# Even and odd columns apart: another layout for the moving operands of a spectral layer and a feed-forward network

## The chip, the core and the metric

The kernel runs on one core of a Trainium2 chip, in a single launch. The metric is the device time of one execution in microseconds, the median of several runs. The core has a matrix engine (TensorE, PE in the profile; its weight loads are shown as an engine of their own, PEld), a vector engine (VectorE, DVE), a scalar engine (ScalarE, ACT), GpSimd (POOL), and a sequencer that issues most transfers (SyncE, SP). Matrix products read both operands from the on-chip memory SBUF and write to PSUM.

## The reference

Eight sequences of 3008 tokens with 256 features go through a Fourier layer and then through a feed-forward network:

```python
X = np.fft.rfft(x, axis=1)
Yr = Xr @ w_r - Xi @ w_i + b_r          # float32
Yi = Xr @ w_i + Xi @ w_r + b_i
Y  = softshrink(Yr, 0.01) + 1j * softshrink(Yi, 0.01)
y  = np.fft.irfft(Y, n=3008, axis=1)     # 8 x 3008 x 256
h  = y @ w_in                            # 24064 x 2048
g  = h - np.tanh(h)
out = g @ w_out                          # 24064 x 256
```

`w_in` and `w_out` arrive as float64.

## The kernel before

**Arithmetic.** The precise products are made of three fp32r products. A float32 operand is split into a rounded high part (`_h`, written by ACT as fp32r) and the rest (`_l`, a subtraction on DVE, also written as fp32r), and the product is low·high + high·high + high·low, added up in PSUM. A few products near the start and two transforms (L361, L580) run in full float32; each of these shows as two matmul records in the trace, while an fp32r product shows as one.

**The Fourier part** is done batch by batch in small matrices (3008 = 64 · 47). Class `Stacked` (L278) makes the first transform of batches 1 to 7: `split` rounds a tile `xs` of 94 rows by 2 x 256 columns, `dft` (L301) multiplies it, ACT copies the result out of PSUM into `st` (L304), and a DMA stores `st` to DRAM. Class `Spectrum` makes the second transform, the complex linear layer, the shrinkage and the first half of the inverse; `Chunk.wave` and `Chunk.fold` make the second half of the inverse and leave `yt`, the network's input, with features on the partitions and tokens along the columns.

**The network** works on 52 chunks of tokens, 44 of 470 columns and 8 of 424. `halves` (L598) splits `yt` into `yh` and `yl`. For each of 16 blocks `f` of 128 hidden units, `up` makes six matmuls (L609: `win_l`·`yh`, `win_h`·`yh`, `win_h`·`yl`, two tiles of features each) into a PSUM tile `h`, then ACT makes `th` = tanh (L618), DVE `g` = `h` - `th` (L621), ACT `gh` (L624), DVE `gl` (L627). `down` makes six matmuls (L640: `gh` with `wout_l` and `wout_h`, `gl` with `wout_h`, for two halves of the output), added up over `f` in two PSUM tiles. A chunk and a block together are a slot; there are 832. The tiles `yh`, `yl`, `gh` and `gl` have rows of 512 words (`PITCH`), of which the first 470 or 424 are used, and every matmul reads them as one run of adjacent columns.

**Order.** It is written out by hand: in slot `g` the loop emits `up` of slot `g + 2`, then whatever of the Fourier part was put into this slot by `plan_stacked` and `plan_spectrum`, then `down` of slot `g`. So between the making of `gh` and `gl` and their use lie about two slots. `th`, `g`, `gh` and `gl` have three buffers each. The first slots also carry the conversion of the weights from float64 (class `Block`, L185 to L217), whose inputs are every second word of `w_raw`.

Of the kernel before, what the change touches and what calls it, by code (L numbers as in the profile page):

```python
# [10 lines left out]
F32 = mybir.dt.float32  # L11
# [3 lines left out]
ALU = mybir.AluOpType  # L15

B, S, D, FF = 8, 3008, 256, 2048
# [61 lines left out]
def spectral_ffn(ctx, tc, x, w_r, w_i, b_r, b_i, w_in, w_out, x_twice, f1, f1s, f2, i1, i2, out):  # L79
    nc = tc.nc  # L80
    P = 128
# [14 lines left out]
    ps_h = ctx.enter_context(tc.tile_pool(name="ps_h", bufs=2, space=PSUM))  # L96
    ps_o = ctx.enter_context(tc.tile_pool(name="ps_o", bufs=1, space=PSUM))
    ps_f = ctx.enter_context(tc.tile_pool(name="ps_f", bufs=4, space=PSUM))

    def split(src, name, pool=const, tag=None, bufs=None, rest=nc.vector):  # L100
        hi, lo = pair_like(src, name, pool, tag, bufs)
        split_into(hi, lo, src, rest)
        return hi, lo
# [119 lines left out]
    stack = {}  # L223
# [57 lines left out]
    class Stacked:  # L281
# [15 lines left out]

        def dft(self, q):
            ps = ps_f.tile([P, 512], F32, name="ps_f1", tag="f")
            pv = ps.rearrange("p (a d) -> p a d", d=D)  # L300
            nc.tensor.matmul(pv, stack["r"], self.xs[q], start=True, stop=True)  # L301
            if q == 0:
                self.st = work.tile([96, XC, D], F32, name="st", tag="st")
            nc.scalar.copy(out=self.st[:, 2 * q:2 * q + 2, :], in_=pv[:96])  # L304
            if 2 * q + 2 == XC:
                n = self.ch * XC
                nc.sync.dma_start(out=a_dram[self.b][n:n + XC].rearrange("n r d -> r n d"), in_=self.st)
# [18 lines left out]
    def halves(t, jp):  # L326
        v = t.rearrange("n (u g j) d -> u n g (j d)", u=2, j=NJ)
        return [v[u][:, :, 2 * jp * D:(2 * jp + 2) * D] for u in range(2)]

    class Spectrum:  # L330
# [6 lines left out]
        def load(self):  # L337
            if self.jp == 0:
                z_dram[self.b] = dram.tile([P * NJ, D], F32, name=f"z_{self.b}", tag="z")
            self.at = load.tile([P, 2, D], F32, name="at", tag="at", bufs=3)  # L340
            dst = self.at.rearrange("p j d -> p (j d)")
            if self.b < PAIRED:
                nc.sync.dma_start(out=dst, in_=rows(a_dram[self.b], self.jp))
                return
            first, second = halves(a_dram[self.b], self.jp)
            nc.sync.dma_start(out=dst, in_=first)
            n = 2 * XC * LOOK if self.b == PAIRED else 0
            nc.gpsimd.dma_start(out=dst[2 * n:], in_=second[n:], accum_op=ALU.add)  # L348
# [192 lines left out]
    class Chunk:  # L541
# [55 lines left out]

        def halves(self, t):  # L598
            n, y = self.n, self.y[t]
            nc.scalar.copy(out=self.yh[:, t, :n], in_=y[:, :n])  # L600
            nc.vector.tensor_tensor(out=self.yl[:, t, :n], in0=y[:, :n], in1=self.yh[:, t, :n].bitcast(F32), op=ALU.subtract)  # L601

        def up(self, f, between=()):
            n = self.n
            h = ps_h.tile([P, 512], F32, name="h", tag="h")
            k = 0
            for lhs, rhs in ((win_l, self.yh), (win_h, self.yh), (win_h, self.yl)):
                for t in range(2):
                    nc.tensor.matmul(h[:, :n], lhs[:, t, f * P:(f + 1) * P], rhs[:, t, :n], start=k == 0, stop=k == 5)  # L609
                    k += 1  # L610
            between = dict(enumerate(between))

            def fill(k):
                for op in between.get(k, ()):
                    op()

            th = ffn.tile([P, CT], F32, name="th", tag="th")
            nc.scalar.activation(out=th[:, :n], in_=h[:, :n], func=AF.Tanh)  # L618
            fill(0)
            g = ffn.tile([P, CT], F32, name="g", tag="g")  # L620
            nc.vector.tensor_tensor(out=g[:, :n], in0=h[:, :n], in1=th[:, :n], op=ALU.subtract)  # L621
            fill(1)
            gh = ffn.tile([P, PITCH], F32R, name="gh", tag="g_h")
            nc.scalar.copy(out=gh[:, :n], in_=g[:, :n])  # L624
            fill(2)
            gl = ffn.tile([P, PITCH], F32R, name="gl", tag="g_l")
            nc.vector.tensor_tensor(out=gl[:, :n], in0=g[:, :n], in1=gh[:, :n].bitcast(F32), op=ALU.subtract)  # L627
            fill(3)
            return gh, gl

        def down(self, f, gh, gl):
            n = self.n
            if f == 0:
                if self.c == 1:
                    self.o = [ps_f.tile([P, 512], F32, name=f"o{t}", tag="f") for t in range(2)]
                else:
                    self.o = [ps_o.tile([P, 512], F32, name=f"o{t}", tag=f"o{t}") for t in range(2)]
            for t in range(2):
                for k, (lhs, rhs) in enumerate(((wout_l, gh), (wout_h, gh), (wout_h, gl))):
                    nc.tensor.matmul(  # L640
                        self.o[t][:, :n], lhs[:, f, t * P:(t + 1) * P], rhs[:, :n],
                        start=f == 0 and k == 0, stop=f == NF - 1 and k == 2,
                    )

# [19 lines left out]
    with tc.manual_schedule(engines={E.PE, E.Activation, E.DVE, E.Pool, E.SP}):  # L664
# [21 lines left out]
        for i in range(len(steps) + 1):  # L686
            if i < len(steps):
                steps[i][0].whole(steps[i][1])
            if i >= 1:
                f, q = steps[i - 1]  # L690
# [136 lines left out]
        p, q = blocks[:2]  # L827
# [21 lines left out]
        for k, g in ((2, 3), (4, 8), (6, 13), (8, 18)):  # L849
            p, q = blocks[k:k + 2]  # L850
# [9 lines left out]
        for g in range(-2, FIXED):  # L860
            c, f = steps[g + 2]
# [6 lines left out]
            if g >= 0:  # L868
                c, f = steps[g]
# [52 lines left out]
    for g in range(FIXED, len(order)):  # L922
        if g + AHEAD < len(order):
            c, f = order[g + AHEAD]
# [3 lines left out]
        c, f = order[g]  # L928
# [39 lines left out]
```

## Time and profile before

| | |
|---|---|
| median of 3 runs | 2638.91 us (2638.36 to 2639.53) |
| the profiled execution | 2640.23 us |
| its span, first to last instruction | 2638.5 us |
| PE busy | 2625.8 us, 14098 matmuls |
| DVE busy | 1872.1 us (71%) |
| ACT busy | 1512.5 us (57%) |
| POOL busy | 115.4 us (4%) |
| granted TensorE clock, mean over the span | 0.999 |

In the page, the share of an engine is the time in which at least one of its instructions was under way. Matmuls overlap: the next one starts while the last columns of the one before still run through the array. A busy PE therefore says little on how fast it goes; that is read from the distance between the starts of two matmuls. The duration of one matmul in a group is that distance plus a tail.

### The profile page before, as it was taken

How to read it: one execution, taken by the hardware profiler on the slowest of the kernel's cores; microseconds unless marked ns; L12 is line 12 of the kernel's file. 1: busy time of each engine (PE TensorE's matmuls, PEld its weight loads, DVE VectorE, ACT ScalarE, POOL GpSimd, SP SyncE). 2: the span in 40 equal slices, each digit the busy share in tenths (PEclk: the TensorE clock that was granted, in tenths of full speed). 3: DMA queues.
4: the chain of work that ended last, by engine and by line, in shares of the span. 5: the costliest groups of instructions: out<-in, count | busy, mean ns of one | idle time of the engine just before them, and what ended most of it. 6: DMA issues, size and time to landing. Idle time of an engine off the chain costs nothing.

```text
span 2638.5 us, 38650 instructions
## 1 busy us (share of the span) xinstructions
PE 2625.8 (100%) x14098; PEld 2388.1 (91%) x14098; DVE 1872.1 (71%) x3431; ACT 1512.5 (57%) x2958; POOL 115.4 (4%) x132
## 2 busy tenths in 40 slices
PE   9999999999999999999999999999999999999999
PEld 7789999999999999999999999999999999999888
DVE  5896887677867776767776777667777677755555
ACT  4675568555765556755576555675558555544444
POOL 2110000000000000000000000000000000000000
PEclk9999999999999999999999999999999999999999
DMA  8643326322462312632155221452316422111000
GB/s 239 173 136 93 81 67 192 76 70 63 119 167 67 71 43 80 182 75 70 47 153 137 71 66 39 116 160 61 78 40 180 103 71 62 32 29 29 22 15 15
DMA packets 157543, 236.70 MB, mean 90 GB/s; under 512 B 12561, under 2 KB 108585, under 8 KB 157353
## 3 DMA queue, kind: packets, MB, share of 16 engines
q1 hardware_dynamic: 146025, 213.79, 28.1%
q0 software_dynamic: 11328, 20.45, 5.2%
q8 instruction: 111, 1.82, 0.3%
q14 instruction: 79, 0.65, 0.1%
HBM read 138.77 MB, written 95.42 MB: 89 GB/s over the span
## 4 chain that ended last, share of the span: by engine, by line
PE 95%; DVE 2%; DMA 1%; ACT 1%; issue 1%; SPq 0%; DVEq 0%; ACTq 0%
PE o L640 38%; PE h L609 38%; PE ps_v L381 5%; PE ps_i L580 3%; PE ps_f L361 3%; PE ps_t L381 2%; PE ps_f L301 2%; PE ps_i L429 1%; PE ps_i L428 1%; PE ps_i L427 1%; DMA xt<-in_x 1%; DVE gl L627 0%; ACT gh L624 0%; PE ps_v L483 0%; PE ps_f L252 0%
## 5 line engine op out<-in xcount | busy, mean ns | idle before, releaser
L621 DVE TENSOR_TENSOR g<-h,th 128x470 f32<-128x470 f32 (+1 forms) x832 | 530.7, 638 | 389.2 <-ACT th L618 382.4
L618 ACT ACTIVATE th<-h 128x470 f32<-128x470 f32 (+1 forms) x832 | 464.0, 558 | 587.7 <-PE h L609 584.6
L627 DVE TENSOR_TENSOR gl<-g,gh 128x470 fp32r<-128x470 f32 (+1 forms) x832 | 533.8, 642 | 260.6 <-ACT gh L624 250.3
L624 ACT CAST gh<-g 128x470 fp32r<-128x470 f32 (+1 forms) x832 | 483.8, 581 | 365.7 <-DVE g L621 362.1
L640 PE MATMUL o<-gh,wout_l 128*128 128x470 f32 (+1 forms) x1664 | 624.2, 375 | 0.0
L640 PE MATMUL o<-gl,wout_h 128*128 128x470 f32 (+1 forms) x1664 | 616.7, 371 | 0.0
L640 PE MATMUL o<-gh,wout_h 128*128 128x470 f32 (+1 forms) x1664 | 616.2, 370 | 0.0
L609 PE MATMUL h<-yh,win_l 128*128 128x470 f32 (+1 forms) x1664 | 483.4, 371 | 0.8 <-DVE g L621 0.6
L609 PE MATMUL h<-yl,win_h 128*128 128x470 f32 (+1 forms) x1664 | 482.0, 370 | 0.0
L609 PE MATMUL h<-yh,win_h 128*128 128x470 f32 (+1 forms) x1664 | 480.2, 370 | 0.0
L609 PEld LDWEIGHTS h<-yh,win_l 128*128 128x128 f32 x1664 | 311.8, 188 | 37.8 <-DVE g L621 3.0
L640 PEld LDWEIGHTS o<-gl,wout_h 128*128 128x128 f32 x1664 | 312.8, 188 | 35.8 <-DVE gl L627 1.8
L609 PEld LDWEIGHTS h<-yl,win_h 128*128 128x128 f32 x1664 | 312.6, 188 | 32.6 <-DVE yl L601 0.4
L609 PEld LDWEIGHTS h<-yh,win_h 128*128 128x128 f32 x1664 | 312.6, 188 | 32.4
L640 PEld LDWEIGHTS o<-gh,wout_h 128*128 128x128 f32 x1664 | 313.2, 188 | 31.5
L640 PEld LDWEIGHTS o<-gh,wout_l 128*128 128x128 f32 x1664 | 313.5, 188 | 27.1 <-DVE ot L657 0.2
L296 DVE TENSOR_TENSOR xs<-xt,xs 47x512 fp32r<-47x512 f32 x208 | 139.8, 681 | 40.5 <-ACT xs L295 37.7
L412 DVE TENSOR_TENSOR y<-tb,ps_v 64x256 f32<-64x256 f32 x384 | 160.3, 417 | 7.2 <-ACT tb L499 2.2
L348 POOL DMA_DIRECT2D at<-a x84 | 80.0, 1020 | 1780.7 <-DMA at<-a 1114.6
L295 ACT CAST xs<-xt 94x512 fp32r<-94x512 f32 x208 | 127.9, 626 | 8.8 <-DMA xt<-in_x_twice 8.6
L304 ACT COPY st<-ps_f 96x512 f32<-96x512 f32 x208 | 117.6, 577 | 1.0 <-PE ps_f L301 1.0
L580 PEld LDWEIGHTS ps_i<-i,zin 120*128 120x128 f32 (+1 forms) x832 | 99.4, 192 | 3.0 <-ACT st L304 1.0
(115 smaller groups left out, 2447.0 us busy)
## 6 DMA issues: line engine op xcount, KB each, us to landing
xt<-in_x_twice SPq DMA_DIRECT2D x104, 384.0 KB
a<-st SPq DMA_DIRECT2D x104, 384.0 KB
at<-a SPq DMA_DIRECT2D x96, 256.0 KB
z<-zo SPq DMA_DIRECT2D x93, 240.0 KB
out<-ot SPq DMA_DIRECT2D x44, 470.0 KB
zin<-z SPq DMA_DIRECT2D x42, 480.0 KB
at<-a POOLq DMA_DIRECT2D x72, 256.0 KB, 5.1
turn<-in_i SPq DMA_DIRECT2D x96, 128.0 KB
```

The source lines that it names most:

```text
L295: nc.scalar.copy(out=xs, in_=src)
L296: nc.vector.tensor_tensor(out=xs[:47], in0=src[:47], in1=xs[:47].bitcast(F32), op=ALU.subtract)
L304: nc.scalar.copy(out=self.st[:, 2 * q:2 * q + 2, :], in_=pv[:96])
L381: nc.tensor.matmul(dst, lhs[:, t], rhs[:, t, :], start=n == 0, stop=n == 5)
L412: nc.vector.tensor_tensor(out=y[ri * 64:(ri + 1) * 64, jj, :], in0=common(jj, ri), in1=self.side(ri)[jj * 64:(jj + 1) * 64], op=ALU.add,)
L580: nc.tensor.matmul(ps[:, at:at + m], self.zt[:m, k, t * P:(t + 1) * P], i2t[:m, turn:turn + m], start=True, stop=True,)
L609: nc.tensor.matmul(h[:, :n], lhs[:, t, f * P:(f + 1) * P], rhs[:, t, :n], start=k == 0, stop=k == 5)
L618: nc.scalar.activation(out=th[:, :n], in_=h[:, :n], func=AF.Tanh)
L621: nc.vector.tensor_tensor(out=g[:, :n], in0=h[:, :n], in1=th[:, :n], op=ALU.subtract)
L624: nc.scalar.copy(out=gh[:, :n], in_=g[:, :n])
L627: nc.vector.tensor_tensor(out=gl[:, :n], in0=g[:, :n], in1=gh[:, :n].bitcast(F32), op=ALU.subtract)
L640: nc.tensor.matmul(self.o[t][:, :n], lhs[:, f, t * P:(t + 1) * P], rhs[:, :n], start=f == 0 and k == 0, stop=f == NF - 1 and k == 2,)
```

## The change

Four small helpers describe the layout. `streams` is a view of a tile's row as two runs, the first at word 0 and the second at word 256, each of n/2 words; `moving` is the same view with the two runs read in turn, one word of each; `paired` and `apart` are the views of an ordinary row as pairs, and as all even columns followed by all odd ones.

`halves` and `up` write `yh`, `yl`, `gh` and `gl` in the two runs: even columns in the first, odd ones in the second, 256 words or 1024 bytes further on. The casts and subtractions therefore read `yt` and `g` with a step of two words, and write two runs. The matmuls of `up` and `down` take one column of the first run and one of the second in turn, so the columns reach the array in the same order as before, and the results in PSUM lie as before.

`Stacked.dft` leaves `xs` as it is, two rows of 256 words, so 1024 bytes apart, and reads column 0 of the first, column 0 of the second, column 1 of the first, and so on. Its result in PSUM then lies in pairs, and the copy to `st` (L304) reads PSUM with a step of two words to put the order right.

```diff
+    def streams(t, n):
+        return t.rearrange("p (j i) -> p j i", j=2)[:, :, :n // 2]
+
+    def moving(t, n):
+        return streams(t, n).rearrange("p j i -> p i j")
+
+    def paired(t, n):
+        return t[:, :n].rearrange("p (i j) -> p i j", j=2)
+
+    def apart(t, n):
+        return paired(t, n).rearrange("p i j -> p j i")
...
         def dft(self, q):
             ps = ps_f.tile([P, 512], F32, name="ps_f1", tag="f")
-            pv = ps.rearrange("p (a d) -> p a d", d=D)
-            nc.tensor.matmul(pv, stack["r"], self.xs[q], start=True, stop=True)
+            pv = ps.rearrange("p (d a) -> p d a", a=2)
+            nc.tensor.matmul(pv, stack["r"], self.xs[q].rearrange("p a d -> p d a"), start=True, stop=True)
...
-            nc.scalar.copy(out=self.st[:, 2 * q:2 * q + 2, :], in_=pv[:96])
+            nc.scalar.copy(out=self.st[:, 2 * q:2 * q + 2, :], in_=pv[:96].rearrange("p d a -> p a d"))
...
         def halves(self, t):
             n, y = self.n, self.y[t]
-            nc.scalar.copy(out=self.yh[:, t, :n], in_=y[:, :n])
-            nc.vector.tensor_tensor(out=self.yl[:, t, :n], in0=y[:, :n], in1=self.yh[:, t, :n].bitcast(F32), op=ALU.subtract)
+            yh, yl = streams(self.yh[:, t], n), streams(self.yl[:, t], n)
+            nc.scalar.copy(out=yh, in_=apart(y, n))
+            nc.vector.tensor_tensor(out=yl, in0=apart(y, n), in1=yh.bitcast(F32), op=ALU.subtract)
...
-                    nc.tensor.matmul(h[:, :n], lhs[:, t, f * P:(f + 1) * P], rhs[:, t, :n], start=k == 0, stop=k == 5)
+                    nc.tensor.matmul(
+                        paired(h, n), lhs[:, t, f * P:(f + 1) * P], moving(rhs[:, t], n), start=k == 0, stop=k == 5,
+                    )
...
-            nc.scalar.copy(out=gh[:, :n], in_=g[:, :n])
+            nc.scalar.copy(out=streams(gh, n), in_=apart(g, n))
...
-            nc.vector.tensor_tensor(out=gl[:, :n], in0=g[:, :n], in1=gh[:, :n].bitcast(F32), op=ALU.subtract)
+            nc.vector.tensor_tensor(
+                out=streams(gl, n), in0=apart(g, n), in1=streams(gh, n).bitcast(F32), op=ALU.subtract,
+            )
...
-                        self.o[t][:, :n], lhs[:, f, t * P:(t + 1) * P], rhs[:, :n],
+                        paired(self.o[t], n), lhs[:, f, t * P:(t + 1) * P], moving(rhs, n),
```

No engine gets another instruction, loses one or gets them in another order, and all tiles keep their places in memory. Two things beside the operands change. Line numbers move by 12 to 17. And some waits go, because the framework then finds them implied by others: the subtraction `gl` had, in 483 of its 832 places, a second wait, for the matmuls that read the buffer's last content. On DVE, at a place in the middle of the program, there stood (L621 makes `g`, L627 `gl`, L401 and L402 belong to the shrinkage, L110 splits a result of it):

```order
L621 TENSOR_TENSOR g<-h,th 128x470 [waits Activation_49]
L401 TENSOR_SCALAR mn<-y 128x512 [waits DVE_49]
L402 SCALAR_TENSOR_TENSOR mn<-y,mn 128x512 [waits DVE_49]
L627 TENSOR_TENSOR gl<-g,gh 128x470 [waits PE_49,Activation_49]
L110 TENSOR_TENSOR z_2_l<-mn,z_2_h 128x512 [waits Activation_49]
```

and now, with the same instructions under their new line numbers:

```order
L636 TENSOR_TENSOR g<-h,th 128x470 [waits Activation_49]
L413 TENSOR_SCALAR mn<-y 128x512 [waits DVE_49]
L414 SCALAR_TENSOR_TENSOR mn<-y,mn 128x512 [waits DVE_49]
L642 TENSOR_TENSOR gl<-g,gh 128x2x235 [waits Activation_49]
L122 TENSOR_TENSOR z_2_l<-mn,z_2_h 128x512 [waits Activation_49]
```

The order is the same; `gl` is written as 2 x 235 columns and waits for ACT alone.

## Rows read from the trace of the kernel before

**Rows 1.** The page: busy time of each engine, and its chain by line.

```profile
PE 2625.8 (100%) x14098; PEld 2388.1 (91%) x14098; DVE 1872.1 (71%) x3431; ACT 1512.5 (57%) x2958; POOL 115.4 (4%) x132
...
PE 95%; DVE 2%; DMA 1%; ACT 1%; issue 1%; SPq 0%; DVEq 0%; ACTq 0%
PE o L640 38%; PE h L609 38%; PE ps_v L381 5%; PE ps_i L580 3%; PE ps_f L361 3%; PE ps_t L381 2%; PE ps_f L301 2%; PE ps_i L429 1%; PE ps_i L428 1%; PE ps_i L427 1%; DMA xt<-in_x 1%; DVE gl L627 0%; ACT gh L624 0%; PE ps_v L483 0%; PE ps_f L252 0%
```

**Rows 2.** Waits of PE, the two longest: total us, times, longest.

```profile
PE ps_t L495 <- DVE sf L465: 2.4, 1, 2.4
PE idle L673 <- DVE column L677: 2.0, 1, 2.0
```

**Rows 3.** Timeline of PE, network alone, then beside other work: start us, us.

```profile
1526.93 0.37 PE L640 MATMUL o<-gh,wout_l 128*128 128x470 f32 x1
...
1531.97 0.40 PE L381 MATMUL ps_v<-w_h,xl 128*128 128x256 f32 x2
...
1532.68 0.38 PE L640 MATMUL o<-gh,wout_l 128*128 128x470 f32 x1
...
1533.96 0.58 PE L609 MATMUL h<-yh,win_l 128*128 128x470 f32 x2
```

**Rows 4.** Groups of PE by shape: count, busy us, mean ns, idle before.

```profile
L640 PE MATMUL o<-gh,wout_h 128*128 128x470 f32 x1408 | 525.4, 373 | 0.0
L609 PE MATMUL h<-yh,win_l 128*128 128x470 f32 x1408 | 413.3, 374 | 0.8 <-DVE g L621 0.6
L640 PE MATMUL o<-gh,wout_h 128*128 128x424 f32 x256 | 90.8, 354 | 0.0
L301 PE MATMUL ps_f<-xs,f_stack 94*128 94x512 f32 x208 | 78.2, 396 | 0.2
L381 PE MATMUL ps_v<-w_l,xh 128*128 128x256 f32 x336 | 67.5, 282 | 0.0
L531 PE MATMUL ps_i<-mn,turn 128*128 128x256 f32 x48 | 12.3, 379 | 0.0
```

**Rows 5.** Timeline of PE, six fp32r products of 256 columns and what follows.

```profile
1520.44 0.40 PE L381 MATMUL ps_v<-w_h,xl 128*128 128x256 f32 x2
...
1521.15 0.37 PE L640 MATMUL o<-gh,wout_l 128*128 128x470 f32 x1
```

**Rows 6.** Timeline of PE, full float32 products of 256 columns and what follows.

```profile
61.80 1.89 PE L483 MATMUL ps_v<-w_f,xf 128*128 128x256 f32 x8
63.53 1.03 PE L483 MATMUL ps_t<-wr_f,sf 128*128 128x256 f32 x4
64.39 1.03 PE L531 MATMUL ps_i<-mn,turn 128*128 128x256 f32 x4
65.25 1.05 PE L361 MATMUL ps_f<-f,at 128*128 128x128 f32 x8
```

**Rows 7.** Timeline of PE early on: ten fp32r products of 512 columns.

```profile
23.75 2.43 PE L673 MATMUL idle<-warm 128*128 128x512 f32 x10
```

**Rows 8.** Windows: busy us (count) of PE, PEld, DVE, ACT, POOL; clock; DMA.

```profile
22.00:27.00 5.00, 5.00 (x24) 4.09 (x23) 2.78 (x6) 0.11 (x1) 0.00 (x0) 1.00 0.52 151
100.00:200.00 100.00, 98.49 (x460) 83.18 (x459) 89.72 (x154) 74.32 (x140) 13.91 (x10) 1.00 0.50 145
200.00:500.00 300.00, 300.00 (x1663) 276.11 (x1662) 227.26 (x414) 184.36 (x367) 15.29 (x19) 1.00 0.40 106
```

**Rows 9.** Timeline of a slot's work after `up`, and its first use.

```profile
1528.83 0.59 ACT L624 CAST gh<-g 128x470 fp32r<-128x470 f32 x1 [1.08 <-DVE g L621]
...
1529.78 0.64 DVE L627 TENSOR_TENSOR gl<-g,gh 128x470 fp32r<-128x470 f32 x1
...
1533.11 0.38 PE L640 MATMUL o<-gl,wout_h 128*128 128x470 f32 x1
```

**Rows 10.** Groups of DVE by shape: count, busy us, mean ns, idle before.

```profile
L401 DVE TENSOR_SCALAR mn<-y 128x512 f32<-128x512 f32 x84 | 35.1, 418 | 0.3
L209 DVE SCALAR_TENSOR_TENSOR w_s<-w_raw,w_s 128x512 uint32<-128x512 uint32 x16 | 12.0, 749 | 0.0
L206 DVE SCALAR_TENSOR_TENSOR w_f<-w_raw,w_m 128x512 f32<-128x512 uint32 x16 | 11.0, 685 | 0.1
L212 DVE SCALAR_TENSOR_TENSOR w_f<-w_f,w_s 128x512 f32<-128x512 f32 x16 | 10.8, 682 | 0.1
L188 DVE TENSOR_SCALAR w_s<-w_raw 128x512 uint32<-128x512 uint32 x16 | 6.7, 421 | 1.5 <-DMA w_raw<-in_moe_w_in 1.5
```

**Rows 11.** Line L627: its waits on the sequencer, and what its idle time ended with.

```profile
L627 DVEq EVENT_SEMAPHORE  x483: 21/21/21, 110.5 to 2631.7; - x161
...
  ACT gh L624: 250.3, 386
  PE o L640: 0.7, 1
```

**Rows 12.** Windows of line L627 alone: DVE busy us (count), clock, DMA.

```profile
100.00:200.00 100.00, 26.08 (x36) 1.00 0.50 145
200.00:500.00 300.00, 59.83 (x94) 1.00 0.40 106
```

**Rows 13.** Group of ACT: the copy of the first transform out of PSUM.

```profile
L304 ACT COPY st<-ps_f 96x512 f32<-96x512 f32 x208 | 117.6, 577 | 1.0 <-PE ps_f L301 1.0
```

## The prediction

> **What bounds the kernel now.** I read the page first. PE has work under way all the time, and of the chain that ended last 95% is PE; `down` (L640) and `up` (L609), the two lines that the change is about, have 38% each, the first transform L301 has 2% [rows 1]. Then the waits: PE's two longest in the whole run come to 2.4 and 2.0 us [rows 2], so nothing is won by making an operand ready earlier. The time is the number of matmuls times the distance between their starts, and only that distance is worth looking at.
>
> The distance comes from the timeline. In a stretch with the network alone, 24 matmuls of 470 columns start between 1526.93 and 1531.97: 5.04 us / 24 = 210.0 ns each [rows 3]. The mean duration of such a matmul is 373 to 374 ns [rows 4], so the tail that a duration has beyond the distance is 163 ns. It is the same for other shapes: six fp32r products of 256 columns take 0.71 us, 118.3 ns each [rows 5], at 282 ns duration [rows 4]; so distances can be read off the groups as duration less 163. That gives 210.5 ns for 470 columns, 191 for 424, 233 for the 512 of L301.
>
> [...] One column per cycle would be 195.8 ns for 470, 176.7 for 424, 213.3 for 512, 106.7 for 256. The excess is 14.7, 14.3, 19.7 and 11.6 ns. Where does it come from?
>
> [...]
> - Not from loading weights or changing from one matmul to the next as such: the products in full float32, each record with its own weight load, go at 3.45 us / 16 = 215.6 ns [rows 6] for 256 columns. That is 0.84 ns a column, half the pace of fp32r, and only 2.3 ns above 512 cycles.
> - Hardly from other engines: in the idle loop near the start, where ACT is busy for 0.11 us of 5 and DVE does 6 operations [rows 8], ten fp32r products of 512 columns end 2.43 us after the first one's start [rows 7]; less the tail that is 226.7 ns each, 13.4 above 213.3. Next to other work the same 470-column matmul takes (1533.96 - 1532.68) / 6 = 213.3 ns against 210.0 [rows 3], so at most 3 ns of it come and go with the neighbours.
>
> What is left is that these matmuls take a fresh four-byte column from SBUF in every cycle, and those without the excess take one in two cycles. The excess appears with the full pace of the read, and the read of the moving operand is what the change touches.
>
> **The change part by part.**
>
> *The matmuls of `up`, `down` and L301.* Their number stays. Six groups with 1408 matmuls of 470 columns each make 8448, six with 256 make 1536 of 424 columns, and there are 208 of L301 [rows 4]. After the change a matmul reads from two places 1024 bytes apart, and each place is asked for a column only every second cycle: the pace at which rows 6 show no excess. No row shows a moving operand read so at one column per cycle, so the price is bounded from both sides:
>
> - Best: the excess falls to the 2.3 ns of rows 6. Distances become 198.1, 179.0 and 215.6. Saved: 12.4 x 8448 + 12.3 x 1536 + 17.4 x 208 = 104.8 + 18.9 + 3.6 = 127 us.
> - A smaller gain: only the part that grows with the columns goes. From 256 to 470 columns the distance grows by (210.0 - 118.3) / 214 = 0.4285 ns a column against 0.4167. Saved: 5.6 x 8448 + 5.0 x 1536 + 6.0 x 208 = 47 + 8 + 1 = 56 us.
> - Worst: two places in turn are not served at full pace, and a column costs what it costs in rows 6, 0.84 ns. Distances become 395, 356 and 430: added 184.5 x 8448 + 165 x 1536 + 197 x 208 = 1559 + 253 + 41 = 1853 us.
>
> I take a value near the best, since rows 6 and 7 differ in nothing that I can see but the pace of the read, and leave another 2 ns for what came and went with the neighbours: 200.0, 181.0 and 217.6 ns. Saved: 10.5 x 8448 + 10.3 x 1536 + 15.4 x 208 = 88.7 + 15.8 + 3.2 = 108 us.
>
> [...]
>
> *The casts `gh`, `yh` and the subtractions `gl`, `yl`.* They read with a step of two words and write two runs. On DVE the trace has this step: L188 reads every second word of `w_raw` and takes 421 ns for 512 columns, L401 reads adjacent ones and takes 418; with two inputs L206, one of them so spaced, takes 685, L212 682, though L209 takes 749 [rows 10]. I take nothing; the upper bound is 67 ns by L209, or, on no row at all, a doubled duration: 0.64 us more for `gl` and 0.59 us for `gh` [rows 9], since ACT has no row with such a step. What hides it is the distance to the first use. The `gl` begun at 1529.78 is done at 1530.42 and wanted at 1533.11, 2.69 us later [rows 9]; 1.23 us fit in it even in the worst case. The engines themselves have room too: in 200 to 500 us DVE is busy 227 of 300 us [rows 8] with 94 `gl` [rows 12], and 94 x 0.64 would make it 287.
>
> *The copy L304* reads PSUM with a step of two words, which no row shows. It takes 577 ns, 208 times [rows 13]; doubled, it adds 120 us to ACT's 1512, beside PE, and holds a PSUM buffer of a pool of four 0.6 us longer. I take nothing.
>
> *The waits that go.* The sequencer of DVE spends 21 ns on each of the 483 [rows 11], but the idle time before `gl` ended with ACT's `gh` in 250.3 us of it and with PE in 0.7 us [rows 11]. Nothing comes of it on PE.
>
> *What is late next.* Nothing on PE's path: with all distances 5% shorter, two slots shrink by some 0.25 us, which leaves 2.4 us of the 2.69. DVE's share rises from 71 to 74%.
>
> **The sum.** Against the profiled execution: 2640.2 - 108 = 2532 us. The median lies 1.3 us below that execution, so 2531.
>
> **The rivals.**
>
> *Slower: the alternation costs pace.* [...] At the pace of rows 6 the time is 2639 + 1853 = 4490 us. If only each hitch came twice as often, the excess above 2.3 ns would double: + 127 us, 2766. It decides from the first nanosecond, since PE has no slack.
>
> *Same: the excess is not in the order of the read.* It could belong to the change from one fp32r matmul to the next, as a fixed 12 ns or so, or two places 1024 bytes apart may count as one. For it speaks that the excess grows little with the columns, 11.6 ns at 256 and 14.7 at 470 [rows 4, 5]; against it, that full float32 changes as often and pays 2.3 [rows 6]. Then the time stays at 2636 to 2642.
>
> *Slower, by DVE: pace unchanged, the spaced reads dear.* Between 100 and 200 us DVE is busy 89.7 of 100 us [rows 8], with 36 `gl` [rows 12]. At 0.64 us more each that is 113 of 100, and the surplus of 13 us is lost there: 2652. After that DVE stays below 96%, by the 287 of 300 us above. Rows 10 speak against it.
>
> **How the numbers follow.** Forecast (faster, 2531; its own range 2510 to 2590): 0.57. Same: 0.17. Slower by pace: 0.20, of which a quarter near 2766 and the rest far above. Slower by DVE: 0.06. The range from 2508 to 2700 holds the first two and the last and leaves out 0.20. A measurement of this kernel can tell 0.2%, some 5 us, from no change; by these cases faster by more has 0.57, within it 0.17, slower 0.26.
>
> **What would show it.** In the profile after: distances near 200 ns for 470 columns, so durations near 363 in the groups of `up` and `down`, 344 for 424, 381 for L301 (now L313), with the 256-column products unchanged at 282, as a control. `gl` and `gh` at 0.64 and 0.59 us would confirm that the spaced reads are free, and PE's waits would stay at a few us. Durations of 373 mean the second rival, 500 and more the first; PE idle before `down` with releaser `gl` between 100 and 200 us means the third. The forecast is wrong if the 470-column duration does not fall below 371, or if it falls and the time does not.

## The result, and the profile after

The changed kernel takes 2552.16 us (median of 4 runs, 2549.04 to 2553.59) against 2638.64 us (4 runs): a ratio of 0.9671, 95% interval 0.9654 to 0.9688. It is 86.5 us faster; the forecast said 2531 and so 108 us.

The page of the changed kernel, busy time and chain, answers to [rows 1] (`up` is now L622, `down` L657):

```profile
PE 2519.1 (99%) x14098; PEld 2381.1 (93%) x14098; DVE 1969.6 (77%) x3431; ACT 1674.5 (66%) x2958; POOL 116.9 (5%) x132
...
PE 80%; DVE 10%; ACT 6%; issue 2%; DMA 1%; SPq 0%; ACTq 0%; DVEq 0%
PE h L622 32%; PE o L657 32%; PE ps_v L393 4%; PE ps_i L592 2%; PE ps_f L373 2%; ACT gh L639 2%; DVE gl L642 2%; DVE y L424 2%; DVE g L636 2%; PE ps_t L393 2%; PE ps_f L313 1%; ACT th L633 1%; PE ps_f L264 1%; DMA xt<-in_x_twice 1%; PE ps_i L439 1%
```

Three numbers stand out. The chain was 95% PE and is 80%: DVE and ACT now have 16% of it. ACT is busy for 162 us more and DVE for 98 us more, with the same number of instructions. And PE's idle time, span less busy, has gone from 2638.5 - 2625.8 = 12.7 us to 2550.3 - 2519.1 = 31.2.

PE's groups by shape (count | busy us, mean ns | idle before) answer to [rows 4]:

```profile
L657 PE MATMUL o<-gh,wout_h 128*128 128x470 f32 x1408 | 509.9, 362 | 0.0
L622 PE MATMUL h<-yh,win_l 128*128 128x470 f32 x1408 | 400.2, 365 | 10.2 <-DVE g L636 6.7 <-ACT yh L613 3.0
L657 PE MATMUL o<-gh,wout_h 128*128 128x424 f32 x256 | 87.6, 342 | 0.0
L313 PE MATMUL ps_f<-xs,f_stack 94*128 94x512 f32 x208 | 75.9, 385 | 3.9 <-DVE xs L308 3.9
L393 PE MATMUL ps_v<-w_l,xh 128*128 128x256 f32 x336 | 67.4, 282 | 0.0
```

470 columns: 373 to 362 ns. 424: 354 to 342. The first transform: 396 to 385. The products of 256 columns, which the change does not touch, stay at 282. The distance itself is read from PE's timeline (start us, us), network alone, as in [rows 3]:

```profile
1230.73 0.36 PE L657 MATMUL o<-gh,wout_l 128*128 128x470 f32 x1
...
1235.49 0.40 PE L393 MATMUL ps_v<-w_h,xl 128*128 128x256 f32 x2
```

Between them lie 24 matmuls: 4.76 us / 24 = 198.3 ns, where it was 210.0. The pace of a column comes from the starts too (means without stalls, at a granted clock of 1.00). A record of full float32 stands 215.7 ns from the next at 256 columns and 429.2 at 512: (429.2 - 215.7) / 256 = 0.834 ns a column. `up` now takes half of that, (198.33 - 179.16) / 46 = 0.4167 ns, by its groups of 470 and 424 columns. At this pace 470, 424, 512 and 256 columns would be 195.8, 176.7, 213.3 and 106.7 ns; what a distance has above that is the excess, and 2.5 ns of it are left at 470. The distance also varies less: over the whole trace, eight of ten distances after a 470-column matmul of `up` or `down` are 198 or 199 ns, where they ran from 209 to 215.

What went the other way is in the groups of ACT and DVE (same columns), which read 587 and 651 ns before for `gh` and `gl`:

```profile
L639 ACT CAST gh<-g 128x470 fp32r<-128x470 f32 x704 | 557.9, 792 | 432.7 <-DVE g L636 426.8
...
L316 ACT COPY st<-ps_f 96x512 f32<-96x512 f32 x208 | 118.9, 585 | 0.9 <-PE ps_f L313 0.9
```

```profile
L642 DVE TENSOR_TENSOR gl<-g,gh 128x470 fp32r<-128x470 f32 x704 | 549.6, 781 | 338.9 <-ACT gh L639 334.2
L636 DVE TENSOR_TENSOR g<-h,th 128x470 f32<-128x470 f32 x704 | 455.2, 647 | 106.0 <-ACT th L633 99.3
```

The cast `gh` takes 205 ns more, `gl` 130; `g`, which reads and writes as before, is unchanged, and the copy that reads PSUM with a step takes 8 ns more (577 to 585, [rows 13]). PE now waits more: not for `gh` and `gl` themselves (0.5 us for `gl`), but for other work of the same two engines. Its longest waits (total us, times, longest), where the longest were 2.4 and 2.0 [rows 2]:

```profile
PE h L622 <- DVE g L636: 7.2, 17, 0.9
PE ps_f L313 <- DVE xs L308: 3.9, 8, 0.9
PE h L622 <- ACT yh L613: 3.0, 7, 0.5
```

The windows show where; the columns are those of [rows 8]:

```profile
100.00:200.00 100.00, 90.41 (x408) 71.57 (x408) 87.39 (x136) 70.83 (x122) 15.58 (x10) 1.00 0.40 114
200.00:500.00 300.00, 296.51 (x1700) 284.12 (x1699) 240.89 (x425) 207.06 (x383) 14.52 (x19) 0.99 0.42 114
```

Between 100 and 200 us PE got through 460 matmuls before and 408 now; between 200 and 500 us it got through more, 1700 against 1663 [rows 8].

**The balance.** By the new distances the pace gave 12.2 x 8448 + 12.0 x 1536 + 11 x 208 = 103.1 + 18.4 + 2.3 = 124 us. For the stalls I took each matmul's distance to the next start, less the median distance of the matmuls with the same line, tiles and columns, and added up what was over 25 ns: 25.5 us in the trace before, 62.3 us after, so 37 us more, 16 of them between 100 and 200 us. (PE's idle time shows only half of it, 18.5 us, since the first 163 ns of a stall lie under the tail of the matmul before.) 124 - 37 = 87 us; the two profiled executions differ by 2640.23 - 2552.46 = 87.8.

### The profile page after: what moved, and what is told of

Its sections match the earlier page's. It is cut to its first block, busy times and chain, and to the rows that moved or that the text cites. A ratio compares the mean times of both kernels' runs of the same rounds, so it can differ in the third digit from the quotient of the medians.

```text
span 2550.3 us, 38084 instructions
## 1 busy us (share of the span) xinstructions
PE 2519.1 (99%) x14098; PEld 2381.1 (93%) x14098; DVE 1969.6 (77%) x3431; ACT 1674.5 (66%) x2958; POOL 116.9 (5%) x132
## 4 chain that ended last, share of the span: by engine, by line
PE 80%; DVE 10%; ACT 6%; issue 2%; DMA 1%; SPq 0%; ACTq 0%; DVEq 0%
PE h L622 32%; PE o L657 32%; PE ps_v L393 4%; PE ps_i L592 2%; PE ps_f L373 2%; ACT gh L639 2%; DVE gl L642 2%; DVE y L424 2%; DVE g L636 2%; PE ps_t L393 2%; PE ps_f L313 1%; ACT th L633 1%; PE ps_f L264 1%; DMA xt<-in_x_twice 1%; PE ps_i L439 1%
## 5 line engine op out<-in xcount | busy, mean ns | idle before, releaser
L639 ACT CAST gh<-g 128x470 fp32r<-128x470 f32 (+1 forms) x832 | 652.6, 784 | 460.1 <-DVE g L636 453.8
L642 DVE TENSOR_TENSOR gl<-g,gh 128x470 fp32r<-128x470 f32 (+1 forms) x832 | 639.7, 769 | 386.6 <-ACT gh L639 381.0
L657 PE MATMUL o<-gh,wout_l 128*128 128x470 f32 (+1 forms) x1664 | 606.7, 365 | 3.4 <-DVE ot L674 2.4
L657 PE MATMUL o<-gl,wout_h 128*128 128x470 f32 (+1 forms) x1664 | 599.8, 360 | 1.0 <-DVE gl L642 0.5
L657 PE MATMUL o<-gh,wout_h 128*128 128x470 f32 (+1 forms) x1664 | 597.5, 359 | 0.0
L622 PE MATMUL h<-yh,win_l 128*128 128x470 f32 (+1 forms) x1664 | 467.4, 362 | 10.8 <-DVE g L636 7.2
L622 PE MATMUL h<-yl,win_h 128*128 128x470 f32 (+1 forms) x1664 | 463.3, 360 | 0.1
L622 PE MATMUL h<-yh,win_h 128*128 128x470 f32 (+1 forms) x1664 | 461.7, 359 | 0.0
L622 PEld LDWEIGHTS h<-yh,win_l 128*128 128x128 f32 x1664 | 311.3, 189 | 36.9 <-DVE g L636 14.7
L657 PEld LDWEIGHTS o<-gh,wout_l 128*128 128x128 f32 x1664 | 315.5, 190 | 20.1 <-DVE ot L674 6.4
L657 PEld LDWEIGHTS o<-gl,wout_h 128*128 128x128 f32 x1664 | 314.2, 189 | 21.1 <-DVE gl L642 7.4
L622 PEld LDWEIGHTS h<-yl,win_h 128*128 128x128 f32 x1664 | 313.5, 189 | 15.5 <-DVE yl L614 2.3
L657 PEld LDWEIGHTS o<-gh,wout_h 128*128 128x128 f32 x1664 | 314.8, 189 | 13.9
L622 PEld LDWEIGHTS h<-yh,win_h 128*128 128x128 f32 x1664 | 313.5, 189 | 13.2
L592 PE MATMUL ps_i<-i,zin 120*128 120x120 f32 (+1 forms) x832 | 101.0, 274 | 1.2 <-ACT st L316 1.2
```

Source lines behind the costliest of these rows:

```text
L592: nc.tensor.matmul(ps[:, at:at + m], self.zt[:m, k, t * P:(t + 1) * P], i2t[:m, turn:turn + m], start=True, stop=True,)
L622: nc.tensor.matmul(paired(h, n), lhs[:, t, f * P:(f + 1) * P], moving(rhs[:, t], n), start=k == 0, stop=k == 5,)
L639: nc.scalar.copy(out=streams(gh, n), in_=apart(g, n))
L642: nc.vector.tensor_tensor(out=streams(gl, n), in0=apart(g, n), in1=streams(gh, n).bitcast(F32), op=ALU.subtract,)
L657: nc.tensor.matmul(paired(self.o[t], n), lhs[:, f, t * P:(t + 1) * P], moving(rhs, n), start=f == 0 and k == 0, stop=f == NF - 1 and k == 2,)
```

## The experiments

Two questions were left: what in the new read makes the matmuls faster, and what makes the casts slower. All kernels ran beside the kernel before (medians 2637.9 to 2638.6 us). Where the output columns come in another order, the expectation says so.

### The casts

**e1: separate even and odd where `h` is read from PSUM.** The step is moved from `gh` and `gl` to tanh and `g`; `yh` and `yl` keep it:

```diff
-            nc.scalar.activation(out=th[:, :n], in_=h[:, :n], func=AF.Tanh)
+            nc.scalar.activation(out=runs(th, n), in_=apart(h, n), func=AF.Tanh)
...
-            nc.vector.tensor_tensor(out=g[:, :n], in0=h[:, :n], in1=th[:, :n], op=ALU.subtract)
+            nc.vector.tensor_tensor(out=runs(g, n), in0=apart(h, n), in1=runs(th, n), op=ALU.subtract)
...
-            nc.scalar.copy(out=streams(gh, n), in_=apart(g, n))
+            nc.scalar.copy(out=streams(gh, n), in_=runs(g, n))
...
-                out=streams(gl, n), in0=apart(g, n), in1=streams(gh, n).bitcast(F32), op=ALU.subtract,
+                out=streams(gl, n), in0=runs(g, n), in1=streams(gh, n).bitcast(F32), op=ALU.subtract,
```

`runs(t, n)` is the row as two adjacent runs, 0 to n/2 and n/2 to n.

> The changed kernel, but even and odd columns are separated where tanh and the subtraction g read h from PSUM; gh and gl then read adjacent words and write the two runs. Theory A (the step of two words in SBUF is what made gh 792 and gl 781 ns): gh falls to about 590, gl to about 650, g and th stay at 647 and 564, most of the 37 us of stalls that came go, time 2512 to 2525. Rival B (writing two runs, or the new read of TensorE beside it, made them slow): gh and gl stay near 790 and 780, time about 2550. Rival C: the step costs as much when read from PSUM, th near 770 and g near 780, time about 2550.

Measured: 2524.57 us (4 runs), ratio 0.9571 (0.9557 to 0.9585), 27.6 us better than the changed kernel. Its ACT and DVE groups:

```profile
L642 ACT CAST gh<-g 128x470 fp32r<-128x470 f32 x704 | 412.1, 585 | 366.8 <-DVE g L639 360.9
L636 ACT ACTIVATE th<-h 128x470 f32<-128x470 f32 x704 | 396.0, 562 | 410.1 <-PE h L625 406.1 <-PE ps_f L316 0.8
```

```profile
L645 DVE TENSOR_TENSOR gl<-g,gh 128x470 fp32r<-128x470 f32 x704 | 458.2, 651 | 222.3 <-ACT gh L642 212.8
L639 DVE TENSOR_TENSOR g<-h,th 128x470 f32<-128x470 f32 x704 | 454.4, 646 | 257.7 <-ACT th L636 254.2
```

All four are at their old durations (`th` 562 ns, 564 in the changed kernel). So rival C is out: in e1 the step costs tanh and `g` nothing where they read PSUM. Rival B is out too, since `gh` and `gl` still write two runs beside the new read of TensorE. The casts that kept the step stayed slow (`yh` 585 ns in the kernel before, 798 in the changed one):

```profile
L616 ACT CAST yh<-yt 128x470 fp32r<-128x470 f32 x88 | 69.8, 817 | 12.3 <-DVE yt L611 12.1
```

The stalls by the sum above are 33.2 us, so 29 us of them are gone, and the two profiled executions differ by 2552.46 - 2523.34 = 29.1 us.

**e3, e4: two runs without the step, the step without two runs.**

```diff
# e3: halves of the row, not even and odd columns
-            nc.scalar.copy(out=gh[:, :n], in_=g[:, :n])
+            nc.scalar.copy(out=streams(gh, n), in_=runs(g, n))
# e4: even and odd columns into one run, matmuls as before
-            nc.scalar.copy(out=gh[:, :n], in_=g[:, :n])
+            nc.scalar.copy(out=runs(gh, n), in_=apart(g, n))
```

(`yh`, `yl` and `gl` likewise; in e3 the matmuls read in turn.)

> The kernel before with the two runs 1024 bytes apart, but the casts put the first half of the columns in the first run and the second half in the second, so they read adjacent words; the matmuls of up and down read the runs in turn; output columns in another order; L301 as before. Theory A: gh 590, gl 650, distance 198 ns, time 2514 to 2528 (without the 3 us of L301). Rival B (writing two runs is what costs): gh 790, gl 780, time about 2555.

> The kernel before, where the casts and subtractions to yh, yl, gh and gl read with the step of two words but write one run, and the matmuls read it as before; output columns in another order. Theory A: gh 790 and gl 780 ns as in the changed kernel, distance 210 ns, time 2645 to 2665: a part of the 37 us, since slots are 6% longer and hide more. Rival B: gh and gl as before, 587 and 650, time 2639.

Measured: e3 2524.82 us, ratio 0.9570 (0.9556 to 0.9584), `gh` 585 and `gl` 650 ns. e4 2639.14 us, ratio 1.0004 (0.9995 to 1.0014), `gh` 622 and `gl` 651. e3 came out as theory A has it and speaks against rival B: two runs alone cost nothing. e4 missed theory A: the step alone costs `gh` 35 ns and `gl` nothing, nearly what rival B expected there. So neither is enough by itself; it takes more than one thing.

**e9, e11: the second run 940 or 960 bytes on.**

```diff
# e9
-        return t.rearrange("p (j i) -> p j i", j=2)[:, :, :n // 2]
+        return t[:, :n].rearrange("p (j i) -> p j i", j=2)
# e11
+        return t[:, :480].rearrange("p (j i) -> p j i", j=2)[:, :, :n // 2]
```

> The changed kernel, but the second run begins right behind the first, at word n/2 (940 bytes on for 470 columns), so the casts read with the step of two words and write one run; the matmuls read the two places in turn, output in the right order. The first four runs showed that the step alone (gh 622, gl 651) and two runs alone (585, 650) cost little. Theory A2 (step and two runs together cost): gh about 622, gl about 651, distance 198, time 2522 to 2530. Rival E (the step collides with TensorE's reading in turn): gh near 790, gl near 780, time about 2550.

> The changed kernel with the second run at word 240 (960 bytes on) in place of word 256: casts read with the step of two words and write two runs with a gap of 5 words between them (28 for 424 columns). Theory A3 (a read with a step and a write of two separate runs in one instruction are what is slow): gh near 790, gl near 780, time about 2550. Rival K (it is the 1024 bytes, in the write or against TensorE's read): gh near 640, gl near 653 as with 940 bytes, time 2522 to 2530.

Measured: e9 2525.31 us, ratio 0.9570 (0.9556 to 0.9584), `gh` 639 and `gl` 653 ns; e11 2522.11 us in one execution, `gh` 639 and `gl` 652. The group of ACT in e11:

```profile
L639 ACT CAST gh<-g 128x470 fp32r<-128x470 f32 x704 | 449.7, 639 | 369.4 <-DVE g L636 366.8
```

e11 still reads with the step and writes two runs with a gap, so theory A3 is out and rival K came true: it is the distance of 1024 bytes, with the step. (The step itself still costs `gh` some 50 ns, 639 against 587; e4 had 35.) After e9 alone one would have dropped rival E, that the step collides with TensorE's read; but e9 also changed the distance. The trace of the changed kernel settles it. Its timeline around 1225 us (start us, us) has one `gh` beside the 256-column products, and the next beside `down`:

```profile
1224.55 0.40 PE L393 MATMUL ps_v<-w_h,xl 128*128 128x256 f32 x2
1224.56 0.62 ACT L639 CAST gh<-g 128x470 fp32r<-128x470 f32 x1
...
1225.26 0.36 PE L657 MATMUL o<-gh,wout_l 128*128 128x470 f32 x1
...
1225.55 0.88 ACT L639 CAST gh<-g 128x470 fp32r<-128x470 f32 x1
```

0.62 us beside other matmuls, 0.88 us beside those that read two places 1024 bytes apart. Over all 704 casts of 470 columns: 39 that ran with under 5% of their time beside `up` or `down` took 629 ns on average, 487 that ran with over 95% beside them took 824. For `gl` it is 649 (92 of them) and 803 (508). In e11, where the places are 960 bytes apart, the same split gives 629 and 638. Neither a step beside another distance (e11) nor adjacent words beside this distance (e3, `gh` 585 ns) is slowed.

One rival is left by these runs: wherever a cast was slow, it also wrote its own two runs 1024 bytes apart. The conversion of the weights settles it. It reads `w_raw` with the step and writes one run, and no kernel changed it; it took 685 ns in the kernel before [rows 10]. In the changed kernel, and in e11:

```profile
L218 DVE SCALAR_TENSOR_TENSOR w_f<-w_raw,w_m 128x512 f32<-128x512 uint32 x16 | 12.0, 751 | 0.0
```

```profile
L218 DVE SCALAR_TENSOR_TENSOR w_f<-w_raw,w_m 128x512 f32<-128x512 uint32 x16 | 11.0, 686 | 0.2
```

In the changed kernel the 6 of them with under 5% of their time beside `up` or `down` took 690 ns, the 9 with over 95% beside them 792; in e3, where the casts have no step but the matmuls read the same two places, 688 and 859; in e11 688 and 685. So an SBUF read with a step of two words was slower beside TensorE's read of two places 1024 bytes apart, with two runs written (629 to 824 ns) and with one (690 to 792). Why 1024 stays open.

### The matmuls

**e2: two places 940 bytes apart, nothing else.**

```diff
+    def moving(t, n):
+        return t[:, :n].rearrange("p (j i) -> p i j", j=2)
```

in the kernel before, used for the operand of `up` and `down` alone.

> The kernel before, where only the matmuls of up and down read their row in another order: column 0, column 235, column 1, column 236 and so on, two places 940 bytes apart (848 for 424 columns); casts as before, output columns in another order. Theory A (two places at half pace each): distance 198 ns for 470 columns, duration 361 to 363, time 2512 to 2525. Rival D (it needs the 1024 bytes, places in the same position of two blocks): the distance stays at 210 or rises, time 2640 or more.

Measured: 2524.48 us in one execution. The median distance at 470 columns is 199 ns; one of the groups:

```profile
L643 PE MATMUL o<-gh,wout_h 128*128 128x470 f32 x1408 | 510.1, 362 | 0.0
```

Theory A was met. The 1024 bytes are not needed for the pace. With e1, e3, e9 and e11 this is the fifth kernel at the same pace, all five between 2522 and 2525.5 us: the read order is the gain.

**e10: the same for the linear layer.** On top of e1, the 256-column matrices are stored as even and odd columns, once:

```diff
-                    nc.tensor.matmul(dst, lhs[:, t], rhs[:, t, :], start=n == 0, stop=n == 5)
+                    nc.tensor.matmul(paired(dst, D), lhs[:, t], turns_of(rhs, t), start=n == 0, stop=n == 5)
```

> The kernel of e1_psum_apart, where the matrices of the complex linear layer, moving operands of 256 columns at the line of ps_v and ps_t, are also stored as even and odd columns 1024 bytes apart, once at the start, and read in turn. Theory A (any fp32r operand read from two places goes at full pace): their duration falls from 282 to about 273, 1512 x 9 ns = 14 us, time 2508 to 2513. Rival H (the excess at 256 columns is the cost of changing from one matmul to the next): 282 stays, time 2524.

Measured: 2513.26 us, ratio 0.9524 (0.9508 to 0.9539), the fastest kernel of the study, 11.3 us below e1 and 38.9 below the changed kernel. PE's group:

```profile
L410 PE MATMUL ps_v<-w_l,xh 128*128 128x256 f32 x336 | 65.1, 276 | 0.0
```

It fell from 282 to 276, not to 273; the median distance, from the starts, went from 120 ns in e1 to 112. That is theory A with 11.3 of its 14 us, and just above its range. Some 5 ns above 0.4167 ns a column (106.7) are left, of the 11.6 before, where 470 columns keep 2.5: a part of the excess at 256 columns does not go with the order of the read, which is what rival H said of all of it. Where that part lies is not shown.

**e5, e6: ten places, and a step.**

```diff
# e5
+        return t[:, :n].rearrange("p (j i) -> p i j", j=10 if n % 5 == 0 else 8)
# e6
+        return t[:, :n].rearrange("p (i j) -> p j i", j=5 if n % 5 == 0 else 4)
```

> The kernel before, where the matmuls of up and down read ten places of their row in turn (188 bytes apart; eight places 212 bytes apart for 424 columns); casts as before, output columns in another order. Theory A (what counts is that one place is asked at a lower pace): distance 198 ns or less for 470 columns, time 2520 to 2526. [...]

> The kernel before, where the matmuls of up and down read with a step of five words (20 bytes; four words, 16 bytes, for 424 columns), five or four sweeps over the row; casts as before, output columns in another order. [...] Theory A in its narrow form (one place swept at full pace keeps the excess): 210 ns, 2638.

Measured, one execution each: e5 4620.8 us, e6 4678.2. The group of `up` in e5:

```profile
L612 PE MATMUL h<-yh,win_h 128*128 128x470 f32 x1408 | 715.4, 602 | 0.0
L612 PE MATMUL h<-yh,win_h 128*128 128x424 f32 x256 | 117.2, 549 | 0.0
```

Distances, from the starts, are 414 ns for ten places and 418 for the step of five words at 470 columns, 367 for eight places and 382 for the step of four words at 424: 0.87 to 0.90 ns a column, above the 0.84 of full float32 [rows 6]. Theory A, as "one place is asked at a lower pace", is wrong: ten places ask each at a tenth and take twice the time. In its narrow form it fell with e6: 418 ns, not 210.

**e12, e13, e14: four places, pairs, and a swap within each four words.** All three have two places in turn at 470 columns; 424 columns are read in another order each, in e14 every four neighbours as 0, 2, 1, 3:

```diff
# e12
+        return t[:, :n].rearrange("p (j i) -> p i j", j=4)
# e13
+        return t[:, :n].rearrange("p (j i r) -> p i j r", j=2, r=2)
# e14
+        return t[:, :n].rearrange("p (i a b) -> p i b a", a=2, b=2)
```

> The kernel before, where the matmuls of up and down read two places 940 bytes apart in turn for 470 columns, and four places 424 bytes apart in turn for 424 columns; output columns in another order. [...] Rival L (four places still go, ten were too many or too close): 179 ns or less, time about 2524.

> The kernel before, where the matmuls of up and down read two places in turn for 470 columns, and for 424 columns two columns of one place, two of the other (848 bytes apart) and so on; output columns in another order. Theory A (each place at half pace on average): 179 ns at 424, time about 2524. Rival N (only a change of place at every column helps): 192 ns as in the kernel before, time about 2544; or more where a pair counts as a burst of one place.

> [...] Rival O (it is the 8-byte word, two words 8 bytes apart do as well as two places): 179 ns, time about 2524. Rival P (any column not behind the one before costs a fetch): about 380 ns, time about 2830.

Measured, one execution each: 2595.57, 2663.37 and 2542.11 us. The group of `up` at 424 columns in e12, e13 and e14:

```profile
L614 PE MATMUL h<-yh,win_h 128*128 128x424 f32 x256 | 79.3, 393 | 0.0
```

```profile
L614 PE MATMUL h<-yh,win_h 128*128 128x424 f32 x256 | 91.3, 442 | 0.0
```

```profile
L614 PE MATMUL h<-yh,win_h 128*128 128x424 f32 x256 | 69.9, 354 | 0.0
```

By the starts, a matmul of 424 columns is 226 ns from the next with four places, 271 with pairs, 192 with the swap, against 192 in the kernel before and 179 with two places in turn. Four places came neither to rival L's 179 nor to the 367 of eight places. Pairs ask each place at half pace on average and are slower than one run: theory A's 179 missed, and of rival N only the words "or more" were met. The swap came out at the 192 of the kernel before; rivals O and P missed.

One description of the orders goes with all seven distances: take the columns at even positions of the read and those at odd positions apart, and see where the next column of each lies. With two places in turn it lies right behind the last (179). With one run, or the swap, each has two of every four words (192). With four places each changes between two places (226), with pairs the same with both in one place at a time (271), with eight places each changes among four (367), and with the step of four words its next column lies eight words on (382). That TensorE reads the two apart is the author's estimate from these distances; no run shows it, and it gives no sizes. That four places and pairs differ by 45 ns was not expected by any theory here.

## Why the prediction was right, and where it was not

**What bounds the kernel** was right: the time follows the distance between matmuls. e2 changes the order of that read alone and moves the whole kernel by 113 us.

**The price of the matmuls** was right in kind and a little low. 198.3, 179 and 222 ns were measured against 200.0, 181.0 and 217.6 taken, 124 us against 108; only L313 gained less than was taken. No run shows the clock's rate, on which the forecast's one column per cycle rests; in its place the runs showed 0.4167 ns a column, which gives the same 195.8, 176.7, 213.3 and 106.7 ns. (The sum counts 10.3 ns saved at 424 columns where 191 - 181.0 is 10.0, half a microsecond in all.) The extra 2 ns left for the neighbours were not needed: over the whole trace eight of ten distances are 198 or 199 ns. The reason given, that each place is asked at half the pace, is not sufficient: e5, e12 and e13 ask each place at half the pace or less and lose (414 ns at 470 columns, 226 and 271 at 424). The rows could not tell; they had no row of any such read. That the one order tried was the good one was so far luck.

**The casts priced at nothing** is the step that failed. It took L188 and L206 [rows 10] as rows for a read with a step of two words. They are right for what they show, and e4 agrees (`gl` 651, `gh` 622), but they ran beside matmuls that read one run; in the changed kernel L206 itself, now L218, takes 751 ns in place of 685. Of the price, 205 and 130 ns, all but some 50 ns of `gh` exists only beside the new read of TensorE at 1024 bytes. It was inside the upper bound named (a doubled duration).

**The cover of 2.69 us** [rows 9] held in the quiet slots and not elsewhere: stalls rose by 37 us, 16 of them between 100 and 200 us, where DVE had been busy for 89.7 of 100 us [rows 8]. There the conversion of the weights is slowed as well, which the change does not touch and the forecast did not price: its four reads of `w_raw` take 28 us of DVE in this stretch in place of 23. The forecast named that stretch in its last rival, as costing 13 us, but only as a case in which the pace does not change. It came along with the gain. "What is late next: nothing" was wrong with it: late next is `g`, which has to read `h` before its PSUM buffer is free again (7.2 us of PE's waits above, 1.6 in e1).

**The number** came within 22 us by two errors that partly cancel: the pace gave 16 us more than was taken, and the stalls took 37 that were priced at nothing.

**The copy from PSUM** (577 to 585 ns) came out nearly as priced. **The waits that go** had nothing to give: e2 keeps all 483 of them and has the whole gain.

**The rivals.** That the alternation costs pace fell for two places and is real for other orders: its 395 ns a matmul and 4490 us are 414 ns and 4621 us in e5. That the excess is not in the order of the read fell with e2 at 470 columns; at 256 columns a part of it is true (e10).

## What to carry to other kernels

Where PE bounds and fp32r matmuls stand further apart than 0.417 ns a column, the pace measured here at a granted clock of 1.00, try reading the moving operand from two places in turn, column by column; not in pairs and not from more places, which lost here. Choose the distance by what runs beside it: with 940 or 960 bytes the stepped casts took 639 ns on ACT and 652 to 653 on DVE, with 1024 they took 792 and 781 and cost this kernel 27 us. If a layout has to be taken apart, do it where PSUM is read: in e1 the step was free there on ACT (562 ns) and DVE (646).

## What the runs showed of the hardware that was not expected

- Another engine's read of SBUF was slower beside one read of the moving operand: a cast with a step of two words took 629 ns beside other matmuls and 824 beside matmuls that read two places 1024 bytes apart; a DVE instruction with such a read and an ordinary write went from 690 to 792. The matmuls themselves kept their 198 ns.
- Reading in pairs from two places (271 ns for 424 columns) is slower than one run (192), and two places in turn (179) faster.
- A step of two words cost tanh and the subtraction nothing where they read it from PSUM (562 and 646 ns in e1).
